# Pooled and banded attention with a gated MLP on one core: one batch instead of two on TensorE by groups, no fill matmuls, and a newly searched instruction order

## The chip, the cores and the metric

The kernel runs on one core of one Trainium2 chip. The metric is the device time of one execution in microseconds. The kernel before takes 767.54 us (median of 3 runs, 767.11 to 768.03). In what follows PE is TensorE, DVE is VectorE, ACT is ScalarE, POOL is GpSimd and SP is SyncE, which here only issues DMAs.

## The reference, cut to what matters

Attention over 8 batches and 8 heads (576 tokens, head dimension 64) is the sum of two softmax attentions: one over q, k and v averaged over four neighbouring tokens and then repeated four times, and one over the band of keys fewer than 4 tokens away. The result, 4608 rows of 512, goes through a gated MLP without an activation function.

```python
def _attn_ref(q, k, v) -> np.ndarray:
    ...
    q_d = q.reshape(B, H, Sd, factor, D).mean(axis=3)
    ...
    out_up = np.repeat(sm_attn(q_d, k_d, v_d), factor, axis=2)
    mask = np.abs(pos[:, None] - pos[None, :]) < factor
    scores = np.where(mask, scale * np.matmul(q, k.transpose(0, 1, 3, 2)), -1000000000.0)
    ...
    return (out_up + np.matmul(attn, v)).astype(np.float32)

def _moe_ref(x, w1, w2, w3, w_out) -> np.ndarray:
    a = x @ w1
    b = x @ w2
    h = a * b @ w3
    return (h @ w_out).astype(np.float32)
```

## The kernel before

**The work and its pieces.** The 4608 rows are cut into 24 units of 192 rows (a third of a batch each), and two units make a chunk of 384 rows, so there are 12 chunks, numbered 0 to 11. A batch `b` gives units `3*b` to `3*b+2`. For every unit the band attention is computed, the pooled attention of its batch is added, and the sum is written as two parts, `xh` (the high bits) and `xl` (the rest), so that three fp32r matmuls replace one exact one (`three`, L308 to L310). The MLP of a chunk (`moe`) has eight blocks: for each, 24 gate matmuls into `pab` (12 with w1, 12 with w2), then ACT copies `a` out (L1006), DVE multiplies (L1008), ACT takes the high part `gh` (L1013), DVE the low part `gl` (L1015), and 9 down matmuls accumulate into `acc`. w3 and w_out are multiplied together first (`fold`: L412 on PE, result `wphl`), and all weights arrive as float64 words that ACT and DVE turn into floats (L340, L348, L352, L355).

**Two ways to do the band.** A unit outside the batches in `PB` is done by `unit`: q times each of 7 shifted k on DVE (`pr`, L858), sums over the head dimension on DVE (L871) or ACT (L868), a softmax over 7 values (L878 to L893), 7 weighted v on DVE (`pv`, `xl`, L924) or ACT (L916), three of the six additions on DVE (L934) and three by accumulating DMAs on POOL's queue (L932), then a transpose (L938), the pooled part (L945), `xh` (L951) and `xl` (L952). A unit of a batch in `PB` is done by `group_unit`: score matmuls for groups of 16 pooled positions (`se_ps`, L743), mask, maximum, exponent and division on DVE and ACT (L754 to L770), transposes (`te_ps`, L713), value matmuls (`oe_ps`, L786), the pooled part (L795), `xh` and `xl` (L803, L804). Its batch also has its q and k summed over four tokens on DVE (`pooled_sums`, L646 to L674) instead of by accumulating DMAs (L505).

```python
        if n in rests:
            rests[n](n)
        else:
            unit(n)
        if n == 1:
            fold()
            for g in range(3):
                gate_weights(g)
        if n % 2:
            moe(n // 2)
```

**What sets the order.** Every piece is one task of a planner, and the task's place on its engine comes from a table of numbers, `ORDER`, one list for each of ACT, DVE, PE, Pool and SP (L63 on). Each engine works strictly in that order; a task waits there until what it needs is ready, and everything behind it on the engine waits too. The tiles of `unit` live in a pool, `dvp`, that reuses the memory of the pool of the group units, `pep`: the loads of the first `unit` (`q_t`, `kv`) wait until all group work is over.

**Fills.** `warm(WARM)` gives PE 20 matmuls on zeros before the weights arrive. `keep_clock(m, n)` (L395) adds n more, whose zero product goes into an accumulator of the fold, at the places in `IDLE`.

```python
PB = (0, 1)
IDLE = ((3, 1, 10), (4, 1, 15), (6, 1, 2))
```

Of the kernel before, what the change touches and what calls it, by code (L numbers as in the profile page):

```python
# [43 lines left out]
PB = (0, 1)  # L44
# [14 lines left out]
IDLE = ((3, 1, 10), (4, 1, 15), (6, 1, 2))  # L59
# [37 lines left out]
    ),  # L97
    DVE=(
# [1078 lines left out]
```

## Time and profile before

| | |
|---|---|
| median of 3 runs | 767.54 us |
| span of the profiled execution | 764.2 us |
| PE, DVE, ACT, POOL busy | 749.3, 611.3, 543.7, 128.4 us |
| PE weight loads busy | 652.7 us |
| HBM read and written | 80.26 and 9.44 MB |

The span runs from the first to the last instruction; the runs' times are those of whole executions, and their median is 3.3 us longer than this span. Busy time is the time in which at least one instruction of the engine runs, so that overlapping instructions count once. Matmuls overlap, and the duration of one is longer than the distance to the next.

### The profile page before, as it was taken

What the parts mean: (1) busy time and instruction counts of PE and PEld (TensorE: products, weight loads), DVE (VectorE), ACT (ScalarE), POOL (GpSimd) and SP (SyncE); (2) the same over time, 40 slices, a digit from 0 to 9 for tenths busy, and PEclk for the clock granted to TensorE, in tenths of its full rate; (3) what the DMA queues carried; (4) which work ended last, traced back from release to release, by engine and by line L of the source; (5) the groups of instructions that cost most, each with busy time, mean ns of one, the idle gap of its engine ahead of it and who ended that gap; (6) DMA issues with size and microseconds to landing.
All of it is one profiled execution on the core that took longest, in us unless ns stands there. A gap on an engine that the chain in (4) does not pass through costs nothing.

```text
span 764.2 us, 14972 instructions
## 1 busy us (share of the span) xinstructions
PE 749.3 (98%) x5342; PEld 652.7 (85%) x5342; DVE 611.3 (80%) x1063; ACT 543.7 (71%) x2133; POOL 128.4 (17%) x163
## 2 busy tenths in 40 slices
PE   9999999999999999999999999999999999999996
PEld 6544598789999899899988989899998999999995
DVE  4786898457999999999979999999998999973111
ACT  5399769567778878969778689786788888751211
POOL 2120200310110320232012401331022310010000
PEclk9999999999999999999999999999999999999999
DMA  8998962743695555786479647965478644241101
GB/s 280 313 264 263 241 194 61 140 94 118 151 215 138 143 127 156 140 191 158 96 172 206 135 117 187 177 155 131 115 165 196 138 108 124 47 100 21 36 7 42
DMA packets 51463, 111.91 MB, mean 146 GB/s; under 512 B 5548, under 2 KB 19884, under 8 KB 51388
## 3 DMA queue, kind: packets, MB, share of 16 engines
q0 software_dynamic: 15360, 38.94, 30.0%
q1 hardware_dynamic: 35892, 71.75, 29.1%
q8 instruction: 42, 0.69, 0.4%
q14 instruction: 33, 0.27, 0.1%
q10 hardware_dynamic: 136, 0.26, 0.1%
HBM read 80.26 MB, written 9.44 MB: 117 GB/s over the span
## 4 chain that ended last, share of the span: by engine, by line
PE 80%; DMA 10%; ACT 4%; DVE 4%; issue 1%; SPq 0%; POOL 0%; ACTq 0%; DVEq 0%; POOLq 0%
PE pab L308 16%; PE pab L310 16%; PE pab L309 16%; PE acc L308 8%; PE acc L309 8%; PE acc L310 8%; DMA xl<-pv 3%; DMA raw<-in_w_dram 3%; DMA v_w<-in_v_dram 2%; PE s_ps L566 2%; PE o_ps L527 1%; PE t_ps L605 1%; DMA vs<-in_v_dram 1%; PE oe_ps L786 1%; PE accw L412 1%
## 5 line engine op out<-in xcount | busy, mean ns | idle before, releaser
L868 ACT ACTIVATE junk<-pr 128x64 f32<-128x64 f32 x432 | 111.1, 257 | 20.4 <-DVE pr L858 9.0
L916 ACT ACTIVATE pv<-kv,s 128x64 f32<-128x64 f32 x432 | 111.3, 339 | 12.7 <-DVE s L893 9.4
L858 DVE TENSOR_TENSOR pr<-q_t,kv 128x768 f32<-128x768 f32 x126 | 116.9, 950 | 1.0 <-DMA q_t<-in_q_dram 1.0
L308 PE MATMUL acc<-wphl,gh 128*128 128x512 f32 x288 | 114.5, 398 | 0.0
L310 PE MATMUL acc<-wphl,gl 128*128 128x512 f32 x288 | 112.8, 392 | 0.0
L309 PE MATMUL acc<-wphl,gh 128*128 128x512 f32 x288 | 112.8, 392 | 0.0
L932 POOL DMA_DIRECT2D xl<-pv x54 | 48.3, 894 | 360.1 <-DVE xl L934 311.1
L1008 DVE TENSOR_TENSOR a<-pab,a 128x384 f32<-128x384 f32 x96 | 53.2, 554 | 48.5 <-PE pab L310 33.7
L871 DVE TENSOR_REDUCE s<-pr 128x12 f32<-128x768 f32 x90 | 84.5, 949 | 1.0
L1006 ACT COPY a<-pab 128x384 f32<-128x384 f32 x96 | 45.7, 476 | 53.0 <-PE pab L310 46.4
L1013 ACT CAST gh<-a 128x384 fp32r<-128x384 f32 x96 | 48.9, 510 | 45.2 <-PE acc L309 36.9
L868 ACT ACTIVATION_READ_ACCUMULATOR junk<-pr 128x1 f32 x432 | 81.1, 188 | 0.0
L1015 DVE TENSOR_TENSOR gl<-a,gh 128x384 fp32r<-128x384 f32 x96 | 52.8, 552 | 26.5 <-ACT gh L1013 26.0
L924 DVE TENSOR_TENSOR pv<-kv,s 128x768 f32<-128x768 f32 x72 | 67.8, 949 | 0.3
L308 PE MATMUL pab<-xh,w1a 128*128 128x384 f32 x192 | 65.4, 341 | 0.6 <-ACT a L1006 0.6
L308 PE MATMUL pab<-xh,w2a 128*128 128x384 f32 x192 | 64.9, 338 | 1.1 <-ACT a L1006 1.1
L308 PE MATMUL pab<-xh,wb 128*128 128x384 f32 x192 | 65.6, 342 | 0.0
L308 PE MATMUL pab<-xh,wo 128*128 128x384 f32 x192 | 65.2, 339 | 0.1
L310 PE MATMUL pab<-xh,wb 128*128 128x384 f32 x192 | 64.5, 336 | 0.0
L310 PE MATMUL pab<-xh,wo 128*128 128x384 f32 x192 | 64.5, 336 | 0.0
L309 PE MATMUL pab<-xl,wb 128*128 128x384 f32 x192 | 64.5, 336 | 0.0
L310 PE MATMUL pab<-xh,w1a 128*128 128x384 f32 x192 | 64.4, 336 | 0.0
(122 smaller groups left out, 1737.3 us busy)
## 6 DMA issues: line engine op xcount, KB each, us to landing
xl<-pv POOLq DMA_DIRECT2D x54, 384.0 KB, 4.8
raw<-in_w_dram SPq DMA_DIRECT2D x32, 512.0 KB
qks<-in_qk_dram POOLq DMA_DIRECT2D x18, 576.0 KB, 8.0
kv<-in_kw_dram SPq DMA_DIRECT2D x18, 576.0 KB
kv<-in_vw_dram SPq DMA_DIRECT2D x18, 576.0 KB
out_dram<-o_sb SPq DMA_DIRECT2D x29, 256.0 KB
q_t<-in_q_dram SPq DMA_DIRECT2D x18, 384.0 KB
raw<-in_wout_dram SPq DMA_DIRECT2D x8, 512.0 KB
```

The source lines that it names most:

```text
L308: nc.tensor.matmul(out_ps, lhsT=lh, rhs=rh, start=first, stop=False)
L309: nc.tensor.matmul(out_ps, lhsT=lh, rhs=rl, start=False, stop=False)
L310: nc.tensor.matmul(out_ps, lhsT=ll, rhs=rh, start=False, stop=last)
L858: (nc.gpsimd if o in share["qk_pool"] else nc.vector).tensor_tensor(out=T[o], in0=T["q"], in1=T["k"][:, o * D:o * D + nq].rearrange("p (t ...
L868: nc.scalar.activation(out=junk, in_=T[o][:, t], func=AF.Copy, accum_out=T["s"][:, t, o:o + 1])
L871: reds.append(add("DVE", dve_us(nq), lambda o=o: nc.vector.tensor_reduce(out=T["s"][:, :, o], in_=T[o], op=ALU.add, axis=AX.X), [tp], uses ...
L916: nc.scalar.mul(out=T["pv", o][:, tt], in_=T["v"][:, (tt + o) * D:(tt + o + 1) * D], mul=T["s"][:, tt, o:o + 1])
L924: nc.vector.tensor_tensor(out=T["pv", o], in0=T["v"][:, o * D:o * D + nq].rearrange("p (t d) -> p t d", d=D), in1=T["s"][:, :, o].unsqueez ...
L932: t = add("Pool", 0.9, lambda o=o: nc.gpsimd.dma_start(out=T["x"], in_=T["pv", o], accum_op=ALU.add), [t, tm], uses=[hx, h], late=dma_us(1 ...
L1008: tg = add("DVE", dve_us(CT), lambda f=f: nc.vector.tensor_tensor(out=T["a", f], in0=T["p", 1, f], in1=T["a", f], op=ALU.mult), [ta, ends[ ...
L1013: nc.scalar.copy(out=T["gh", f], in_=T["a", f])
L1015: tl = add("DVE", dve_us(CT), lambda f=f: nc.vector.tensor_tensor(out=T["gl", f], in0=T["a", f], in1=T["gh", f].bitcast(F32), op=ALU.subtr ...
```

## The change

`PB` loses batch 1: its three units, 3 to 5, are done by `unit` on DVE and ACT, and its q and k are summed by accumulating DMAs, as for batches 2 to 7. `IDLE` is empty, so the 54 fill matmuls of L395 go; the first 20 on zeros stay. All five lists of `ORDER` are new. Nothing else differs; lines below the table stand four lines further down.

```diff
-PB = (0, 1)
+PB = (0,)
...
-IDLE = ((3, 1, 10), (4, 1, 15), (6, 1, 2))
+IDLE = ()
...
     ACT=(
-        "64 63 65-67 69 68 70-72 74 73 75-79 0-1 3-5 2 81 80 82-86 7 11 6 9 87 17 15 14 13 12 10 88-89 16 24 26 25 94 27 8 95 29 91 30 28 "
...
+        "63 65 64 66-67 69 68 71 70 72-78 5 79 2 80-82 84 83 0 86 85 87 24-25 27 26 3-4 30 89 88 94 6 29 95 28 96 7 15 31 97-98 32 92 100 "
...
```

Three places show what the new lists do. The first is SP, where the loads of the first `unit` stand (`q_t`, `kv`), behind the group units' values (`v_w`). Before:

```order
L696 DMA v_w<-in_v_dram 72x1x512 x3
L486 DMA qks<-in_qk_dram 128x1152
L490 DMA vs<-in_v_dram 72x512
L491 DMA vs<-in_v_dram 56x512
L492 DMA vl<-in_v_dram 16x512
L696 DMA v_w<-in_v_dram 36x1x512 x2
L696 DMA v_w<-in_v_dram 72x1x512 x4
L1043 DMA out_dram<-o_sb 128x512
L1043 DMA out_dram<-o_sb 64x512 x2
L1043 DMA out_dram<-o_sb 128x512
L836 DMA q_t<-in_q_dram 128x768
L840 DMA kv<-in_kw_dram 128x1152
```

And now:

```order
L700 DMA v_w<-in_v_dram 36x1x512 x2
L700 DMA v_w<-in_v_dram 72x1x512
L337 DMA raw<-in_w_dram 128x2x512 x6
L700 DMA v_w<-in_v_dram 72x1x512 x3
L337 DMA raw<-in_w_dram 128x2x512 x2
L494 DMA vs<-in_v_dram 72x512
L495 DMA vs<-in_v_dram 56x512
L496 DMA vl<-in_v_dram 16x512
L840 DMA q_t<-in_q_dram 128x768
L844 DMA kv<-in_kw_dram 128x1152
L848 DMA kv<-in_vw_dram 128x1152
```

The loads of the first `unit` now follow the last weights (`raw`) and the values of the third group unit, ahead of all stores of the output; the values of three more group units are gone from in front of them.

The second place is DVE, from the last low part of a group unit (`xl` from `xf`) to the first product of a `unit` (`pr`). Before, where it is the sixth group unit and chunk 2 is complete:

```order
L804 TENSOR_TENSOR xl_2058<-xf,xh_2057 128x2x192
L572 TENSOR_SCALAR gmx<-gmx 128x4
L1008 TENSOR_TENSOR a<-pab,a 128x384
L588 TENSOR_SCALAR gsm<-gsm 128x4
L589 RECIPROCAL gsm<-gsm 128x4
L1015 TENSOR_TENSOR gl<-a,gh 128x384
L596 TENSOR_TENSOR pexp<-pexp,gsm 128x2x16
L1008 TENSOR_TENSOR a<-pab,a 128x384
L1015 TENSOR_TENSOR gl<-a,gh 128x384
L858 TENSOR_TENSOR pr<-q_t,kv 128x768 x3
```

And now, where it is the third group unit, in the middle of the blocks of chunk 0:

```order
L808 TENSOR_TENSOR xl_1289<-xf,xh_1288 128x2x192
L592 TENSOR_SCALAR gsm<-gsm 128x4
L593 RECIPROCAL gsm<-gsm 128x4
L600 TENSOR_TENSOR pexp<-pexp,gsm 128x2x16
L1019 TENSOR_TENSOR gl<-a,gh 128x384
L1012 TENSOR_TENSOR a<-pab,a 128x384
L575 TENSOR_REDUCE gmx<-s_ps 128x3 x2
L576 TENSOR_SCALAR gmx<-gmx 128x6
L862 TENSOR_TENSOR pr<-q_t,kv 128x768 x3
```

The first product has moved from the end of batch 1's group work to the end of batch 0's, with about as little other work between.

The third place is PE, where the gates of chunk 9 begin (`xh_7087` before, `xh_6912` now). Before, they follow the last gates of chunk 8 (`xh_6295`):

```order
L309 MATMUL pab<-xl_6296,wb 128x384
L310 MATMUL pab<-xh_6295,wb 128x384
L308 MATMUL pab<-xh_7087,w1a 128x384
L309 MATMUL pab<-xl_7088,w1a 128x384
L310 MATMUL pab<-xh_7087,w1a 128x384
```

And now they follow the last down matmuls of chunk 8:

```order
L312 MATMUL acc_6698<-wphl,gh 128x512
L313 MATMUL acc_6698<-wphl,gh 128x512
L314 MATMUL acc_6698<-wphl,gl 128x512
L312 MATMUL pab<-xh_6912,w1a 128x384
L313 MATMUL pab<-xl_6913,w1a 128x384
L314 MATMUL pab<-xh_6912,w1a 128x384
```

Before, 0.29 of chunk 8's down matmuls were left for later, among the gates of chunk 9. Now every chunk's down matmuls all stand ahead of the next chunk's gates, at all eleven boundaries.

## Rows read from the trace of the kernel before

**Rows 1.** The page's first part, busy time of each engine with its share of the span, and two rows of its second part, the busy tenths of DVE and PE in 40 equal slices of the span.

```profile
PE 749.3 (98%) x5342; PEld 652.7 (85%) x5342; DVE 611.3 (80%) x1063; ACT 543.7 (71%) x2133; POOL 128.4 (17%) x163
PE   9999999999999999999999999999999999999996
DVE  4786898457999999999979999999998999973111
```

**Rows 2.** Busy time of each engine by stage: the stretch and its length, then PE, weight loads, DVE, ACT, POOL with their counts, the granted clock, the busy share of the DMA engines and GB/s. The cuts are the start of the MLP of chunk 0, the first `pr` of a `unit`, and the moments at which `xl` of chunks 5 and 9 was written; the last row begins with the gates of chunk 1.

```profile
0.00:93.60 93.60, 89.36 (x710) 50.43 (x711) 65.52 (x160) 66.97 (x174) 20.52 (x37) 1.00 0.93 273
93.60:180.10 86.50, 85.88 (x1044) 75.08 (x1044) 56.69 (x151) 59.66 (x211) 10.19 (x12) 1.00 0.53 138
180.10:372.60 192.50, 192.50 (x1214) 177.41 (x1213) 184.25 (x284) 156.72 (x684) 36.87 (x43) 1.00 0.61 143
372.60:592.30 219.70, 216.91 (x1420) 197.35 (x1422) 204.18 (x318) 175.42 (x744) 45.39 (x53) 1.00 0.70 159
0.00:592.30 592.30, 584.64 (x4383) 500.28 (x4387) 510.63 (x907) 458.76 (x1811) 112.96 (x145) 1.00 0.68 169
...
163.70:764.20 600.50, 589.82 (x3780) 541.38 (x3777) 495.87 (x773) 426.93 (x1777) 97.66 (x114) 1.00 0.55 129
```

**Rows 3.** The instructions in order of time (start, length, engine, line, operation): the second low part of chunk 9 on DVE, the first gate matmul of chunk 9 on PE, and the last two down matmuls of chunk 11.

```profile
591.34 0.96 DVE L952 TENSOR_TENSOR xl<-xt,xh 128x768 fp32r<-128x768 f32 x1 [0.39 <-ACT xh L951]
...
597.41 0.34 PE L308 MATMUL pab<-xh,w1a 128*128 128x384 f32 x1
...
756.32 0.39 PE L309 MATMUL acc<-wphl,gh 128*128 128x512 f32 x1
756.54 0.39 PE L310 MATMUL acc<-wphl,gl 128*128 128x512 f32 x1
```

**Rows 4.** The chain of waits between 106 and 116 us, where group matmuls of batch 1 stand in it (start, length on the chain, what), and the group of the fill matmuls (busy time in all, mean ns of one).

```profile
106.08 0.90 PE se_ps L743 x23
...
110.37 0.65 PE te_ps L713 x6
...
114.84 1.48 PE oe_ps L786 x96
...
L395 PE MATMUL accw<-ident,still 128*128 128x128 f32 x54 | 6.6, 277 | 0.0
```

**Rows 5.** PE's instructions in order of time at three moments of the opening: the first matmuls on zeros, the fold where it waits for a weight, and the value matmuls of the second group unit where they wait for `v_w`.

```profile
1.13 7.59 PE L387 MATMUL accw<-still 128*128 128x128 f32 x40 [1.13 <-DVE still L290]
...
34.51 1.98 PE L412 MATMUL accw<-wo,w 128*128 128x512 f32 x4 [1.36 <-DVE w L355]
...
86.44 1.32 PE L786 MATMUL oe_ps<-pte,v_w 72*32 72x64 f32 x80 [0.60 <-DMA v_w<-in_v_dram]
```

**Rows 6.** Groups of DVE instructions of a `unit`, 18 units in all: first the products and the sums, then the longest of the eight groups of 768 columns, then two of the softmax's small steps (count, busy time, mean ns of one).

```profile
L858 DVE TENSOR_TENSOR pr<-q_t,kv 128x768 f32<-128x768 f32 x126 | 116.9, 950 | 1.0 <-DMA q_t<-in_q_dram 1.0
L871 DVE TENSOR_REDUCE s<-pr 128x12 f32<-128x768 f32 x90 | 84.5, 949 | 1.0
L938 DVE STREAM_TRANSPOSE xt<-xl 128x768 f32<-128x768 f32 x18 | 17.5, 972 | 1.2 <-DMA xl<-pv 1.1
L890 DVE TENSOR_REDUCE sm<-s 128x12 f32<-128x96 f32 x18 | 4.5, 248 | 1.2 <-ACT s L886 1.2
L892 DVE RECIPROCAL sm<-sm 128x12 f32<-128x12 f32 x18 | 4.1, 228 | 0.5
```

**Rows 7.** Groups of DVE instructions of the two batches done by groups: the five longest and the shortest of fourteen.

```profile
L754 DVE TENSOR_TENSOR se<-se_ps,band 128x216 f32<-128x216 f32 x24 | 8.2, 376 | 3.6 <-PE se_ps L743 3.5
L795 DVE TENSOR_TENSOR xf<-oe_ps,oup 128x192 f32<-128x192 f32 x24 | 7.5, 352 | 9.5 <-PE oe_ps L786 8.9
L770 DVE TENSOR_TENSOR se<-se,esm 128x432 f32<-128x432 f32 x12 | 7.3, 605 | 0.2
L763 DVE TENSOR_REDUCE emx<-se 128x6 f32<-128x432 f32 x12 | 7.2, 598 | 0.3
L804 DVE TENSOR_TENSOR xl<-xf,xh 128x384 fp32r<-128x384 f32 x12 | 6.7, 556 | 2.3 <-ACT xh L803 2.2
...
L509 DVE COPY vl<-vl 16x512 f32<-16x512 f32 x2 | 0.8, 418 | 0.1
```

**Rows 8.** DVE in order of time at the hand-over from groups to units: the last low part of a group unit, and the first three products of a `unit`.

```profile
171.87 0.55 DVE L804 TENSOR_TENSOR xl<-xf,xh 128x384 fp32r<-128x384 f32 x1
...
180.14 2.69 DVE L858 TENSOR_TENSOR pr<-q_t,kv 128x768 f32<-128x768 f32 x3
```

**Rows 9.** What DVE waited for (us in total, times, longest): three rows of the stretch from 180 to 592.3 us, and the first row of the stretch from 180 to 372.6 us.

```profile
DVE a L1008 <- PE pab L310: 5.9, 11, 1.0
DVE xl L934 <- DMA xl<-pv: 4.4, 2, 3.4
DVE gl L1015 <- ACT gh L1013: 2.2, 5, 0.6
...
DVE a L1008 <- PE pab L310: 2.9, 5, 1.0
```

**Rows 10.** The accumulating DMAs of the units, from the page's sixth part: count, size, median us from issue to landing.

```profile
xl<-pv POOLq DMA_DIRECT2D x54, 384.0 KB, 4.8
```

**Rows 11.** Two stretches of 1 us behind the last matmul, columns as in rows 2.

```profile
760.00:761.00 1.00, 0.00 (x0) 0.00 (x0) 0.00 (x0) 0.00 (x0) 0.00 (x0) 1.00 0.51 178
...
762.00:763.00 1.00, 0.00 (x0) 0.00 (x0) 0.00 (x0) 0.00 (x0) 0.00 (x0) 0.50 0.21 82
```

176 rows, old and new, of tables (ACT, DVE, PE, Pool) are left out of this document.

## The prediction

> **What bounds the kernel now.** I read the page's first part, then the stages, then two engines in order of time. The first part shows PE busy 749.3 us of 764.2 and DVE 611.3 [rows 1]. The stages say where DVE's free time lies [rows 2]. Until 93.6 us, when chunk 0 begins, the DMA engines are at 0.93 and DVE idles 93.6 - 65.52 = 28.1 us: the opening is set by loads, and PE itself waits for a weight and for `v_w` [rows 5]. From 93.6 to 180.1 PE is full and DVE idles 29.8 us, because no `unit` may start before the groups of batch 1 are done. From 180.1 to 592.3 PE is full (409.4 of 412.2) and DVE nearly so: idle 8.25 of 192.5, then 15.5 of 219.7. At the end of that stretch `xl` of chunk 9 is ready at 592.3 and its gates start at 597.41 [rows 3]: 5.1 us spare. So PE sets the end, with DVE close behind it, and DVE's only large reserve is the stage before 180 us. The slices show DVE nearly empty again in the last 70 us [rows 1], but nothing can move there, since the MLP of chunk 11 needs all units done.
>
> **The change part by part.** *PE.* A group unit costs two score blocks of 0.90, two flips of 0.65 and one value block of 1.48: 4.58 us [rows 4]. Three go: 13.7 us. The fills go too, 6.6 us [rows 4], but they stand in the opening, beside the waits of 1.36 and 0.60 us [rows 5]; the bounds are 0 and 6.6, and I take 0, because the stage is set by loads and the nearest rows are waits. Had PE stayed the bound, the span would be 764.2 - 13.7 = 750.5, or 743.9 with the fills.
>
> *DVE.* A `unit` has 23 instructions of 768 columns, 0.949 to 0.972, and five small steps of about 0.24 [rows 6]: 23 x 0.951 + 5 x 0.24 + 0.1 (the edge mask, on two units of three) = 23.2 us, three of them 69.6. The group work of one batch is half of fourteen groups, of which the five longest and the shortest are shown [rows 7]; count times mean over all of them gives, for one batch, 31.8. Net 37.8 us. These are summed lengths, and neighbours overlap: three products of 0.950 take 2.69 [rows 8], and over the whole engine counts times means give 668.8 against 611.3 busy [rows 1], a factor 0.914. So DVE gets 34.5 us more to do, and what hid such work before, PE's lead, is the 5.1 us above.
>
> *Where it decides.* I count to the moment when `xl` of chunk 9 is ready. Before, DVE had been busy 510.6 us by then [rows 2]. In the new list 42.8 summed us more stand ahead of it (the 37.8, and 5 of work for later units that now comes earlier), 39.1 in busy time: 549.7. From the gates of chunk 9 to the end it took 764.2 - 597.4 = 166.8. In the new list 6.5 less is left for PE there: 0.29 of a chunk's 72 down matmuls, one every 0.228 on average (the last two start 0.22 apart [rows 3]), 4.8 us, and 1.7 of pooled attention, now stand ahead. That leaves 160.3. With 0.3 from the last low part to the first gate, span = 549.7 + 160.3 + 0.3 + idle = 710.3 + DVE's idle time before that moment. (The same sum for the kernel before: 510.6 + 81.7 idle + 5.1 + 166.8 = 764.2.)
>
> The idle time has three parts. The opening: its loads are almost the same, so 28, with 24 and 30 as bounds; chunk 0 then begins near 87 to 89. The hand-over: the first `unit` loads after the last group unit, and before that took from 171.87 to 180.14, 8.3 us [rows 8], in which DVE had 2.6 of other work; the new list has 2.7 there, so 5.6, and 2.4 for the waits for the third group unit's matmuls: 8. The rest, 463 us busy from the first product to chunk 9: in 180.1 to 372.6, with PE full, DVE idled 8.25, of which 2.9 was waiting for PE's gates [rows 9]. Once DVE is the late one, such waits should mostly go, so 5.3 of 192.5, 2.8%: 13.3 us. Bounds: 2%, 9.4; and the 5.8% of the whole stretch to 592.3 (23.8 of 412.2, waits for PE and all [rows 2]), 28.5.
>
> Sum: 710.3 + 28 + 8 + 13.3 = 759.6. The same path through chunk 1 gives 761: it needs 68.6 busy us after chunk 0's low part, plus 8 and 1, while PE has some 59 us of work for it, so PE should stand idle there for 12 to 16 us; from chunk 1's gates to the end it took 600.5 [rows 2], now 4.7 less by count (87 + 77.6 + 0.3 + 595.8). The two agree within my error. The median of the runs is 767.54, 3.3 above the span, so 759.6 means 762.9: I say 763.
>
> *Hidden.* POOL gets nine more accumulating DMAs of `unit` and three more sums of q and k; it was busy 128.4 us [rows 1], and the DMA engines were at 0.61 to 0.70 after 180 us [rows 2], so bandwidth costs nothing; their latency is a rival. ACT gains 32 summed us by count, some 25 busy, to 543.7 [rows 1] and stays below DVE. On SP, the loads of the first `unit` stand behind eight weight loads and three `v_w`, which must have gone out for the group unit anyway.
>
> **The rivals.** *PE stays the bound.* DVE keeps ahead, because the new lists are made for its load, idling under 1.5%, and chunks come in time. Then the floor above holds, 743.9 to 750.5, in runs 747 to 754. For it: PE without a gap over 192 us [rows 2]. Against: DVE would have to do 34.5 us more in a time 14 shorter, and the hole before chunk 1.
>
> *DVE's waits are not PE's fault (slower).* A unit's three accumulating DMAs hang on one another, 4.8 us each from issue to landing [rows 10]; DVE waited for them 4.4 us and for `gh` from ACT 2.2 [rows 9], at a time when PE held it back and a wait cost nothing. With three more units, and batch 1's sums of q, k and v in between in POOL's queue, DVE stands in these waits with nobody behind to hide them. At 4.3% (all its waits of 180 to 592 but the 5.9 for PE) the third part is 20.8 and a run takes 770.4; at 5.8%, 778. It decides from 4.0%, where a run takes 769.1.
>
> *Nothing to see.* The third part comes to 3.4 to 4.0%, 16.4 to 19.5 us, or the opening loses what the rest gains: 766 to 769, the 13.7 us of PE bought and paid back on DVE.
>
> *The clock.* Behind the last matmul, which ends at 756.9, the granted clock is still 1.00 at 760 and 0.50 at 762 [rows 11], that is 1.2 GHz for 2.4. So the hole before chunk 1 can drop it. Forty matmuls on zeros at the start, most of them at the lower level, took 7.59 us, 0.19 each [rows 5], against 6.6 / 54 = 0.12 for the fills [rows 4]: a drop costs about 40 x 0.07 = 2.7 us. One is hidden while DVE is late. One at each of eleven boundaries, since every chunk now ends with its own down matmuls, would take 30 us: PE's 743.9 to 750.5 become 774 to 780, 777 to 784 in runs. The Trainium skill's page "TensorE: Matmul & The Clock Gate", section "Why this matters for your kernels", warns of idle gaps between bursts of matmuls in mid-kernel, since they put the array back to the slower clock. By that rule taking out fills speaks against the change; the trace agrees in its one long gap, at the end, and shows no drop at the gap of 1.36 us, where the stage's clock is 1.00 [rows 2].
>
> **How the numbers follow.** Faster or slower is told from no change at 0.2%: under 766.0, over 769.1. The forecast, DVE as the bound, 758 to 766: 0.37. PE the bound, 747 to 754, and the space up to 758: 0.17. Nothing to see: 0.18. DVE's waits: 0.25. The clock: 0.03. Faster 0.54, same 0.18, slower 0.28. The range goes from 750 to 775; what it leaves out is the lower half of PE's case and the far ends of the last two. The forecast's own range is 758 to 766.
>
> **What would show it.** Right: PE idle some 23 us up to its last matmul, instead of 756.9 - 749.3 = 7.6, above all 12 to 16 us near 150 to 165, and short gaps where chunks begin; gates starting within 1 us of `xl`; the first product of a `unit` near 122 instead of 180; DVE busy about 646 us and its stages from there above 0.96. Wrong: if PE shows no gaps and `xl` is ready several us before the gates, PE stayed the bound; if DVE's waits for `xl` and `gh` grow past 4%, the slower case; if the first product comes after 130, the hand-over was mis-sized.

## The result and the profile after

The changed kernel takes 772.2 us (median of 4 runs, 771.36 to 773.04), the kernel before, timed beside it, 767.33 (764.55 to 768.03): ratio 1.0065, 95% interval 1.0036 to 1.0094. It is slower; I had forecast 763.0, faster. Three later timings of the same kernel, on three chips, gave 1.0126 (1.0092 to 1.0160), 1.0108 (1.0068 to 1.0148) and 1.0064 (1.0034 to 1.0095). The profiled execution has a span of 769.6 us, 2.6 below the median.

The first part of the profile's page and two rows of its second part, of the kernel after (they answer to [rows 1]; PEclk is the granted clock in tenths):

```profile
PE 739.9 (96%) x4820; PEld 641.0 (83%) x4820; DVE 638.2 (83%) x1066; ACT 558.1 (73%) x2266; POOL 139.2 (18%) x175
DVE  5845778999999999999989999979989989976111
PEclk9998999979999999999999999999999999999999
```

PE lost 20.3 us of work by the prediction's count and shows only 9.4 less busy time (749.3 to 739.9); DVE is full from 125 us on; and the clock has two slices below 9, where before it had none.

Busy time by stage after, columns as in [rows 2]. The cuts are `xl` of chunk 0, the first `pr`, and `xl` of the chunks 1, 5 and 9; the last row begins with the gates of chunk 9:

```profile
0.00:91.00 91.00, 81.71 (x624) 43.80 (x625) 57.03 (x145) 64.08 (x167) 14.41 (x30) 0.96 0.89 265
91.00:125.50 34.50, 32.24 (x310) 26.70 (x309) 26.75 (x60) 25.21 (x72) 3.26 (x4) 1.00 0.61 181
125.50:168.40 42.90, 37.14 (x234) 30.55 (x233) 40.70 (x64) 37.47 (x174) 10.48 (x12) 0.88 0.79 182
168.40:386.00 217.60, 216.24 (x1361) 197.84 (x1360) 209.65 (x333) 179.42 (x792) 51.53 (x61) 1.00 0.71 161
386.00:608.20 222.20, 218.34 (x1428) 198.58 (x1427) 208.03 (x325) 172.49 (x760) 48.33 (x57) 0.99 0.67 152
...
609.40:769.60 160.20, 152.99 (x866) 142.60 (x864) 94.85 (x143) 78.40 (x302) 10.89 (x13) 0.99 0.31 74
```

Behind the stretch and its length stands PE's busy time, and as the third of the busy times DVE's. The prediction's sum was made of these terms, and they are now measured:

| term (us) | predicted | measured |
|---|---|---|
| DVE busy until `xl` of chunk 9 | 549.7 | 542.2 |
| from there to the gates of chunk 9 | 0.3 | 1.2 |
| gates of chunk 9 to the end | 160.3 | 160.2 |
| DVE idle: opening (0 to 91.0) | 28 | 34.0 |
| DVE idle: hand-over (91.0 to 125.5) | 8 | 7.75 |
| DVE idle: the rest (125.5 to 608.2) | 13.3 (2.8%) | 24.3 (5.0%) |
| span | 759.6 | 769.6 |

PE has an account of its own. The same view cut at the gates of chunk 1 and at the last matmul, of the kernel before:

```profile
0.00:163.70 163.70, 159.46 (x1565) 111.35 (x1566) 115.47 (x291) 116.80 (x356) 30.70 (x49) 1.00 0.76 210
163.70:756.90 593.20, 589.79 (x3780) 541.38 (x3777) 495.79 (x773) 426.35 (x1776) 97.66 (x114) 1.00 0.56 129
```

and of the kernel after:

```profile
0.00:169.70 169.70, 152.39 (x1170) 102.12 (x1171) 125.78 (x267) 128.06 (x418) 28.30 (x47) 0.95 0.80 225
169.70:762.40 592.70, 587.47 (x3651) 538.91 (x3649) 512.39 (x800) 429.50 (x1848) 110.91 (x129) 1.00 0.59 135
```

Ahead of chunk 1 PE stood idle 17.3 us instead of 4.2 and ran at half clock, 1.2 GHz for 2.4, in two stretches of 6.9 and 10.2 us, in which it was busy 15.9 us. At most half of that, 7.9 us, is lost to the clock, so by this estimate the work there fell by 15.0 us (159.5 to 152.4 - 7.9 = 144.5), and chunk 1 still began 6.0 us later. Behind it PE's busy time fell by 2.3 us and the stretch by 0.5. So in these two profiles the last matmul came 5.5 us later: 6.0 lost ahead of chunk 1, 0.5 won behind it. Some three quarters of what PE was relieved of stood ahead of chunk 1, whose gates also need DVE's low part of the first `unit`: it was written at 168.4, and they began at 169.7.

The hole ahead of the first half-clock stretch, the three stretches themselves, and the 15 us in which the prediction had PE idle for 12 to 16 (it was idle 4.6), columns as above:

```profile
62.60:67.20 4.60, 0.00 (x0) 0.00 (x0) 3.75 (x9) 3.44 (x11) 0.00 (x0) 1.00 0.94 265
67.20:74.10 6.90, 6.86 (x73) 4.11 (x74) 2.51 (x9) 3.75 (x10) 0.00 (x0) 0.51 0.62 195
...
156.00:166.20 10.20, 9.03 (x78) 5.90 (x77) 9.39 (x17) 7.66 (x30) 0.86 (x1) 0.50 0.65 171
...
524.60:528.00 3.40, 3.40 (x12) 3.35 (x11) 3.06 (x5) 3.34 (x16) 1.85 (x3) 0.51 0.81 133
...
150.00:165.00 15.00, 10.39 (x92) 7.27 (x91) 14.30 (x23) 11.61 (x54) 1.73 (x2) 0.70 0.77 167
```

Each half-clock stretch comes behind a hole on PE. PE's instructions in order of time (start, length, what, idle time before and what ended it): the three holes, the first gates of the chunks 0, 1 and 9, and the last matmul.

```profile
67.24 1.19 PE L531 MATMUL o_ps<-pt,vs 128*32 128x144 f32 x16 [4.64 <-DMA vs<-in_v_dram]
...
94.76 0.74 PE L312 MATMUL pab<-xh,w1a 128*128 128x384 f32 x1
...
154.61 0.44 PE L609 MATMUL t_ps<-ident,pexp 128*128 128x128 f32 x2 [3.44 <-ACT pexp L598]
...
169.73 0.34 PE L312 MATMUL pab<-xh,w1a 128*128 128x384 f32 x1
...
524.07 0.44 PE L312 MATMUL pab<-xh,wo 128*128 128x384 f32 x1 [2.02 <-DVE a L1012]
...
609.39 0.34 PE L312 MATMUL pab<-xh,w1a 128*128 128x384 f32 x1
...
762.00 0.39 PE L314 MATMUL acc<-wphl,gl 128*128 128x512 f32 x1
```

On DVE, in order of time: the first product of a unit ([rows 8] showed it at 180.14), and the last low parts of the chunks 1 and 9 (answering to [rows 3]).

```profile
125.49 0.96 DVE L862 TENSOR_TENSOR pr<-q_t,kv 128x768 f32<-128x768 f32 x1
...
167.43 0.96 DVE L956 TENSOR_TENSOR xl<-xt,xh 128x768 fp32r<-128x768 f32 x1
...
607.28 0.95 DVE L956 TENSOR_TENSOR xl<-xt,xh 128x768 fp32r<-128x768 f32 x1
```

What DVE waited for between 170 and 605 us after, the first three rows and a later one (answering to [rows 9]):

```profile
DVE xl L938 <- DMA xl<-pv: 8.0, 4, 3.6
DVE a L1012 <- PE pab L314: 1.8, 3, 0.9
DVE gl L1019 <- ACT gh L1017: 1.4, 4, 0.5
...
DVE pr L862 <- DMA q_t<-in_q_dram: 0.8, 1, 0.8
```

Waits for PE's gates went from 5.9 to 1.8 us, as predicted; waits for the accumulating DMAs went from 4.4 to 8.0 (in a window of 435 us instead of 412), though one of them now takes 4.2 us from issue to landing, where [rows 10] have 4.8.

What DVE waited for in the opening, until `xl` of chunk 0: the three longest rows before (to 93.6 us) and after (to 91.0), all of them waits for ACT's share of the weights' conversion:

```profile
DVE wo L355 <- ACT wo L340: 8.5, 3, 5.3
DVE wx L355 <- ACT wx L340: 3.6, 3, 1.9
DVE w L355 <- ACT w L340: 3.2, 5, 1.0
...
DVE w L359 <- ACT w L344: 9.1, 6, 3.0
DVE wo L359 <- ACT raw L352: 6.9, 1, 6.9
DVE wx L359 <- ACT wx L344: 6.4, 2, 4.3
```

### The profile page after: what moved, and what is told of

Read it like the earlier page. It is cut to its first block, busy times and chain, and to the rows that moved or that the text cites. A ratio compares the mean times of both kernels' runs of the same rounds, so it can differ in the third digit from the quotient of the medians.

```text
span 769.6 us, 14109 instructions
## 1 busy us (share of the span) xinstructions
PE 739.9 (96%) x4820; PEld 641.0 (83%) x4820; DVE 638.2 (83%) x1066; ACT 558.1 (73%) x2266; POOL 139.2 (18%) x175
## 4 chain that ended last, share of the span: by engine, by line
PE 51%; DMA 17%; DVE 13%; ACT 9%; issue 5%; POOL 1%; SPq 1%; DVEq 0%; ACTq 0%; POOLq 0%
PE pab L312 10%; PE pab L314 10%; PE pab L313 10%; PE acc L312 6%; PE acc L314 6%; PE acc L313 6%; DMA vs<-in_v_dram 5%; DMA raw<-in_w_dram 4%; ACT junk L872 4%; DVE pr L862 4%; PE o_ps L531 2%; DMA xl<-pv 2%; DVE s L875 1%; DMA vl<-in_v_dram 1%; DMA raw<-in_wout_dram 1%
## 5 line engine op out<-in xcount | busy, mean ns | idle before, releaser
L920 ACT ACTIVATE pv<-kv,s 128x64 f32<-128x64 f32 x504 | 132.7, 337 | 15.2 <-DVE s L897 8.9
L872 ACT ACTIVATE junk<-pr 128x64 f32<-128x64 f32 x504 | 129.1, 256 | 16.0 <-DVE pr L862 4.7
L862 DVE TENSOR_TENSOR pr<-q_t,kv 128x768 f32<-128x768 f32 x147 | 135.3, 949 | 2.0 <-ACT junk L872 0.9
L875 DVE TENSOR_REDUCE s<-pr 128x12 f32<-128x768 f32 x105 | 97.9, 946 | 0.3
L872 ACT ACTIVATION_READ_ACCUMULATOR junk<-pr 128x1 f32 x504 | 94.8, 188 | 0.0
L928 DVE TENSOR_TENSOR pv<-kv,s 128x768 f32<-128x768 f32 x84 | 78.5, 949 | 1.3 <-DMA xl<-pv 0.8
L938 DVE TENSOR_TENSOR xl<-xl,pv 128x768 f32<-128x768 f32 x63 | 59.9, 951 | 17.6 <-DMA xl<-pv 12.2
L493 POOL DMA_DIRECT2D vs<-in_v_dram x48 | 50.4, 1150 | 93.1 <-DMA vs<-in_v_dram 91.3
L312 PE MATMUL pab<-xh,w1a 128*128 128x384 f32 x192 | 65.9, 343 | 0.7 <-ACT a L1010 0.5
L313 PE MATMUL pab<-xl,wo 128*128 128x384 f32 x192 | 65.1, 339 | 0.0
```

Of the source, the lines that this page charges most:

```text
L312: nc.tensor.matmul(out_ps, lhsT=lh, rhs=rh, start=first, stop=False)
L313: nc.tensor.matmul(out_ps, lhsT=lh, rhs=rl, start=False, stop=False)
L493: dma = (lambda **kw: nc.gpsimd.dma_start(accum_op=ALU.add, **kw)) if add else nc.sync.dma_start
L862: (nc.gpsimd if o in share["qk_pool"] else nc.vector).tensor_tensor(out=T[o], in0=T["q"], in1=T["k"][:, o * D:o * D + nq].rearrange("p (t ...
L872: nc.scalar.activation(out=junk, in_=T[o][:, t], func=AF.Copy, accum_out=T["s"][:, t, o:o + 1])
L875: reds.append(add("DVE", dve_us(nq), lambda o=o: nc.vector.tensor_reduce(out=T["s"][:, :, o], in_=T[o], op=ALU.add, axis=AX.X), [tp], uses ...
```

## The experiments

Two theories stood at the start. *DVE sets the end* (the prediction's): each us of DVE's work or waits is one of the span, and the loss is the opening and the waits. *PE sets the end*: the holes and the half clock are lost time. A ratio is always to the kernel before, timed beside it on one chip; the groups of runs were on different chips, so kernels of different groups are compared with care. A profile is of one execution.

**The opening: loads and fills.** `o_ps` of batch 0 waits for `vs` and `vl`, whose first loads stand on SP behind 19 weight loads (the expectation says 20). First these loads were moved forward.

```diff
-21-22 5 23-27 6-7 28-31 12 32-38
+21-22 5 12 23-27 6-7 28-38
```

> The changed kernel with one task moved on SP: the first loads of batch 0's values (vs, vl) go out right behind the last of its k4 loads instead of behind 20 weight loads. Loads theory (the late loads make o_ps wait 4.6 us on PE, and DVE, which sets the end, starts its units that much later): o_ps starts near 63 instead of 67.2, no stretch at half clock there, gates of chunk 0 near 90 instead of 94.8, first product of a unit near 121 instead of 125.5, time 4 to 5 us shorter, 767 to 768. PE theory (PE sets the end and the hole counts directly): 3 to 5 us shorter as well, but gates of later chunks then start well behind xl. Fills theory (clock drops for want of fills are the loss): the clock still drops in the opening and the time is within 1 us of the changed kernel's.

Ratio 1.0045 (1.0013 to 1.0077), span 765.1. The hole went, but `o_ps` did not come earlier:

```profile
67.76 0.70 PE L531 MATMUL o_ps<-pt,vs 128*32 128x144 f32 x16
```

PE was busy with products of the fold up to that moment, so the loads theory is wrong as it stood. What changed is the clock: these matmuls took 0.70 us instead of 1.19, and chunk 0's gates came 24.0 us behind `o_ps` (91.8) instead of 27.5 (94.8); chunk 1's at 164.4. Then the fills were put back, with the loads as in the changed kernel:

```diff
-IDLE = ()
+IDLE = ((3, 1, 10), (4, 1, 15), (6, 1, 2))
```

> The changed kernel with the 54 fill matmuls put back behind the products of block 1 with j = 3, 4 and 6. Fills theory: the stretches at half clock go and the time falls by 3 to 5 us. Loads theory: o_ps still waits for vs and vl until 67, the clock still falls behind that wait, the fills lie ahead of it and cost PE 5 to 7 us that it has spare: within 1 us of the changed kernel. PE theory: about 6 us longer.

Ratio 1.0043 (1.0013 to 1.0073), span 770.0. `o_ps` at 67.4 at full clock, chunk 0 at 91.8, chunk 1 at 164.9, all as in the run before; but from there to the end it took 605.1 us, where the changed kernel's four profiles have 599.9 to 603.4. And the fills taken from the kernel before:

> The kernel before without its 54 fill matmuls, all else in place. Fills theory: slower than before by 3 to 5 us, with a stretch at half clock between 30 and 60 us. PE theory: up to 6 us shorter, since PE sets the end and has less to do. Loads theory: within 1 us, because loads set the opening and the fills lie beside waits for them.

Ratio 1.0023 (0.9997 to 1.0049): no difference that can be told. Its profile, of the slowest of its 12 runs, shows half clock at 28.5 to 31.9, 35.3 to 42.2 and 93.4 to 96.8 us, where the kernel before has none, and chunk 0's gates at 100.7 instead of 93.3. To separate the hole from the clock, 34 fills were put into the hole itself, and the changed kernel was run beside it.

```diff
+            if b == 0:
+                for _ in range(34):
+                    nc.tensor.matmul(open_acc[5][:, :128], lhsT=still, rhs=ident, start=False, stop=False)
```

> The changed kernel with 34 fill matmuls (some 4.1 us) on PE right ahead of o_ps of batch 0, that is inside the hole of 4.6 to 5.7 us, and nothing else. Clock theory (the wait itself is cheap, the half clock behind it costs): o_ps still starts at 67 to 68, takes 1.97 us instead of 3.44, gates of chunk 0 come near 92 instead of 95, those of chunk 1 3 to 5 us earlier, time 3 to 5 us shorter than the changed kernel of the same call. Wait theory (the hole itself is the loss): o_ps and all behind it within 1 us of the changed kernel's.

> The changed kernel as it is, a third timing, to compare the other runs of this call with. All theories: ratio to before between 1.004 and 1.013.

1.0112 (1.0066 to 1.0158) against 1.0108 (1.0068 to 1.0148). The hole and the stretch behind it in this run:

```profile
62.60:67.20 4.60, 4.60 (x44) 4.60 (x43) 2.51 (x6) 1.86 (x5) 0.00 (x0) 1.00 1.01 295
67.20:74.10 6.90, 6.90 (x93) 4.59 (x92) 2.13 (x6) 3.46 (x10) 0.00 (x0) 1.00 0.48 150
```

So the clock theory is right on what it says of PE (25.5 us from `o_ps` to chunk 0's gates, 32.5 in the changed kernel beside it; chunk 1 at 164.0 against 173.6), and the time did not follow: from chunk 1 on it took 605.1 us against 601.6, and the two ratios are equal. The two profiles are of executions of 770.9 and 777.0 us, so not all of the 9.6 us at chunk 1 need be the hole's.

A further step took the third group unit's `v_w` and batch 1's first `vs` ahead of the last four weight loads, in the belief that the memory of the first unit comes free only when those weights are converted. What the profiles show is the load of `q_t` waiting for the low part of the third group unit, 9.9 us in the changed kernel and 9.6 in this run.

```diff
-45-50 56-58 51-52 60-63
+45-48 56-58 60 49-52 61-63
```

> The changed kernel with two moves on SP alone: the first loads of batch 0's values right behind the k4 loads (as in the earlier run), and the third group unit's v_w and batch 1's first vs and vl ahead of the last four weight loads instead of between and behind them. Hand-over theory (the last weights release the memory of the first unit, whose first product so starts at 122 to 127; from there DVE has no time to give): last weight conversions at 109 to 110 instead of 113 to 117, first product near 118, gates of chunk 1 near 161, end 4 us before that of the run with the first move alone, time 764 to 766. Balance theory (behind chunk 1 PE and DVE are both full and the gain is lost in new waits): first product near 118 too, but the end within 1.5 us of the run with the first move alone.

Ratio 1.0025 (0.9998 to 1.0052), span 764.4. First product at 121.5, not 118, chunk 1 at 163.9. The price of moving loads was misjudged, the gain over the first move is not shown. It was run again beside the changed kernel:

> The changed kernel as it is, on one chip with the run below. All theories: ratio to before between 1.005 and 1.013.

> The run with the two moves of loads on SP once more, beside the changed kernel on the same chip, since the chips differ. Opening theory (what is lost ahead of chunk 1 reaches the end): gates of chunk 1 4 to 6 us earlier than in the changed kernel's profile, time 0.4 to 0.7% shorter than the changed kernel's. Balance theory: chunk 1 earlier by as much, but the time within 0.2% of the changed kernel's.

1.0042 (1.0016 to 1.0068) against 1.0064 (1.0034 to 1.0095): 1.8 us in the medians, with intervals that overlap; chunk 1's gates were 2.8 us earlier in the profiles. That is between the two theories and settles neither.

**One engine relieved at a time.** The addition of the pooled part in `up` was left out, in the changed kernel and in the kernel before:

```diff
-            nc.vector.tensor_tensor(out=x, in0=x, in1=o, op=ALU.add)
+            pass
```

> The changed kernel without the addition of the pooled part in the units (one DVE instruction of 768 columns, some 0.87 us net, in each of 21 units; that part of the output is left out). DVE theory (DVE sets the end): 17 units stand ahead of chunk 9, so the time falls by 10 to 15 us, to 757 to 762, and PE's gaps shrink. PE theory: within 2 us.

> The kernel before without the addition of the pooled part in its 18 units (that part of the output is left out), the control for the run that did this to the changed kernel. All theories hold that PE sets the end of the kernel before: within 2 us of before, DVE some 13 us less busy and waiting that much longer.

Changed: 1.0036 (1.0007 to 1.0065), some 2 to 7 us better than the changed kernel's four timings, none of which ran beside it; its interval overlaps with two of theirs. Before: 1.0007 (0.9980 to 1.0035), nothing. Then 48 down matmuls, 11.0 us of PE by count; from chunk 1 to the end the profiles show PE 7.4 us less busy in the changed kernel (587.5 to 580.1) and 8.2 in the kernel before (589.8 to 581.6):

```diff
+                    if 2 <= c <= 9 and f in (3, 4):
+                        nc.tensor.matmul(T["acc"][i], lhsT=gh[:, cs], rhs=wphl[:, f, 0], start=False, stop=False)
+                        nc.tensor.matmul(T["acc"][i], lhsT=gl[:, cs], rhs=wphl[:, f, 0], start=False, stop=False)
+                        return
```

> The changed kernel without 48 of its down matmuls (the second of each three, for blocks 3 and 4 of the chunks 2 to 9; that small part of the product is left out): 48 times 0.229 us is 11.0 us less for PE between 220 and 660 us. PE theory (the holes and half-clock stretches ahead of chunk 1 are lost time, and from there PE sets the end): 8 to 11 us shorter. DVE theory (DVE sets the end from there as well): 0 to 2 us shorter, and PE's gaps grow by 9 to 11 us.

> The changed kernel as it is, timed once more beside the runs below. All theories: the ratio to before as in the first timing, 1.004 to 1.009.

> The kernel before without the same 48 down matmuls (that small part of the product is left out), the control for the run that did this to the changed kernel. If PE alone sets the end of the kernel before: 9 to 11 us shorter. If DVE is so close behind that it takes over at once: 3 to 6 us shorter, since xl of chunk 9 had 5.1 us to spare.

Changed: 1.0074 (1.0048 to 1.0100) against 1.0126 (1.0092 to 1.0160) beside it, 3.6 us of those 7.4, with intervals that just overlap; before: 0.9902 (0.9865 to 0.9939), 7.4 us of 8.2. And both cuts together:

> The changed kernel without the 48 down matmuls and without the addition of the pooled part in the units. Both theories: 9 to 13 us shorter than the changed kernel, since both engines have less to do. If a latency that hangs on neither (the accumulating DMAs, one after another) sets the pace: 0 to 5 us.

1.0017 (0.9988 to 1.0047), 8.6 us below the changed kernel beside it. The stretch from chunk 1's gates to those of chunk 9 shows what happened, each time in the profile of that run (length, then PE's busy time first and DVE's third). The kernel before, then without the 48 matmuls, then without `up`:

```profile
163.70:597.40 433.70, 430.29 (x2856) 393.59 (x2854) 400.16 (x623) 346.34 (x1476) 83.80 (x98) 1.00 0.65 152
```

```profile
164.70:591.60 426.90, 423.02 (x2815) 385.06 (x2814) 398.78 (x623) 345.01 (x1474) 83.39 (x98) 1.00 0.65 154
```

```profile
165.00:600.50 435.50, 431.77 (x2857) 395.33 (x2855) 388.65 (x609) 346.51 (x1476) 83.92 (x98) 1.00 0.65 151
```

PE's idle time is 3.4, 3.9 and 3.7 us: the stretch is nearly all PE's work. The changed kernel, then without the matmuls, without `up`, and without both:

```profile
169.70:609.40 439.70, 434.48 (x2787) 396.31 (x2786) 417.58 (x658) 351.68 (x1549) 100.02 (x117) 1.00 0.69 156
```

```profile
166.50:607.10 440.60, 427.69 (x2743) 387.91 (x2744) 417.55 (x659) 353.00 (x1557) 99.87 (x116) 1.00 0.69 156
```

```profile
166.30:605.30 439.00, 433.21 (x2786) 394.61 (x2786) 407.05 (x644) 352.91 (x1557) 100.33 (x117) 1.00 0.69 157
```

```profile
170.10:603.70 433.60, 424.64 (x2745) 386.56 (x2743) 406.19 (x644) 352.37 (x1556) 99.92 (x116) 1.00 0.70 158
```

The stretch keeps its length when PE gets less (PE's idle time goes from 5.2 to 12.9 us) and when DVE gets less (DVE's from 22.1 to 31.9), and shortens by 6.1 only when both do. Single profiles scatter, so two more without either cut, the changed kernel's fourth timing and the run with the filled hole:

```profile
171.20:614.40 443.20, 435.85 (x2786) 396.48 (x2787) 419.52 (x660) 353.74 (x1558) 100.64 (x117) 1.00 0.68 155
...
164.00:608.60 444.60, 435.43 (x2786) 394.26 (x2785) 419.15 (x660) 353.30 (x1556) 100.01 (x117) 1.00 0.68 155
```

Against 439.7 to 444.6 us, one cut alone (440.6 and 439.0) cannot be told from none, and 433.6 stands clear. Neither of the two theories holds alone: both engines stand so near their limit that each bounds the other. Other engines are in it too: in the run without the 48 matmuls PE's longest wait behind chunk 1, 3.9 us before 293.9 for a product of DVE, follows a wait of DVE of 3.9 us that ends at 289.8 behind a copy on ACT.

**Is there a third bound?** The last of a unit's three accumulating DMAs was left out, alone and with both cuts.

```diff
-lambda o=o: nc.gpsimd.dma_start(out=T["x"], in_=T["pv", o], accum_op=ALU.add), [t, tm]
+(lambda: None) if i == 6 else lambda o=o: nc.gpsimd.dma_start(out=T["x"], in_=T["pv", o], accum_op=ALU.add), [t, tm]
```

> The changed kernel without the last of a unit's three accumulating DMAs (that part of the weighted sum is left out); work of PE, DVE and ACT as before. Latency theory (behind chunk 1 the three DMAs that hang on one another set the pace, with little to spare on PE and DVE): 4 to 8 us shorter, DVE's waits for xl<-pv gone or halved. Balance theory (PE, 99% busy there, and DVE, 95%, bound each other): 0 to 3 us shorter.

> The changed kernel without the 48 down matmuls, without the addition of the pooled part in the units, and without the last accumulating DMA. With the first two left out the time was 1.1% shorter, of 11 and 14 us that PE and DVE had less to do. Latency theory: now the rest comes, 4 to 6 us more. Balance theory: within 2 us of the run with the first two.

1.0152 (1.0119 to 1.0185), not faster than the changed kernel beside it (1.0108), rather slower; and 1.0049 (1.0016 to 1.0083) with both cuts, no better than without this one (1.0017). Between the two runs without the third DMA, timed side by side, both cuts again gave 8.7 us (medians 778.6 and 769.8). What DVE waited for between 170 and 605 us in the first of them:

```profile
DVE xl L938 <- DMA xl<-pv: 8.7, 3, 4.4
DVE pr L862 <- DMA q_t<-in_q_dram: 6.4, 3, 2.5
DVE a L1012 <- PE pab L314: 3.1, 5, 1.0
DVE pr L862 <- DMA kv<-in_kw_dram: 2.0, 1, 2.0
```

A third of the accumulating DMAs went and the waits for the others stayed (8.7 us), while waits for the loads of `q_t`, 0.8 us in the changed kernel, grew to 6.4, and those for `kv` came on top. The latency of these DMAs as the pace is not borne out.

**Two holes closed by hand.** PE waited 3.44 us for the last divisions of batch 1's second pooled block, and 2.02 us for a product in chunk 7, at the same places in nearly every profile of this order. On top of the two moves of loads both instructions were put forward in the lists of ACT and DVE:

```diff
-211 236 164-165 237 267 238 265 239-241 264 242 210 263 270 268 273 266 212
+211 210 212 236 164-165 237 267 238 265 239-241 264 242 263 270 268 273 266
...
-817-818 774 808 775 718 717
+817-818 718 717 774 808 775
```

> The kernel of the run before this one, with two more moves: on ACT the last two divisions of batch 1's second pooled block ahead of unit 3's products (PE waited 3.44 us for them near 151 in every run), and on DVE the product a of chunk 7's block 3 and the low part before it three places earlier (PE waited 2.03 us near 522 in every run). Balance theory: each gap goes and little of it reaches the end, 0 to 2 us. PE theory: 5 us less, and the half-clock stretch near 155 gone.

Ratio 1.0051 (1.0028 to 1.0074), against 1.0025 without these edits on the same chip: no gain. PE's instructions at the two places:

```profile
153.22 0.69 PE L531 MATMUL o_ps<-pt,vs 128*32 128x144 f32 x4 [4.34 <-ACT pt L618]
...
527.26 0.50 PE L314 MATMUL acc<-wphl,gl 128*128 128x512 f32 x1 [2.59 <-DVE gl L1019]
```

Both holes went and were paid a few instructions later, 4.34 us for the copies of `pt` and 2.59 for a low part. With the fills on top:

> The same with the 54 fills put back. Clock theory (a hole in the opening drops the clock and chunk 0's gates come some 3 us late; fills prevent it): no half-clock stretch before chunk 0, gates of chunk 0 no later than without fills, 0 to 3 us shorter. Fills only cost where no hole is left: 0 to 3 us longer.

Ratio 1.0067 (1.0042 to 1.0092): no gain either, and half clock at 85.0 to 91.8 and 156.7 to 166.9 all the same. No version of the changed kernel beat the kernel before. The six timings with loads moved or fills put back have ratios of 1.0025 to 1.0067, the changed kernel's four 1.0064 to 1.0126, but the filled hole has 1.0112, and only one of the six ran beside the changed kernel: that a better opening gains something is suggested, not shown.

## Why the prediction was wrong, step by step

- *The sign.* Wrong. The median is 9.2 us above the forecast of 763.0; the time lies in the range of 750 to 775.
- *DVE becomes the late one, and gates start within 1 us of `xl`.* The lag at chunk 9 is 1.2 us. But that it is then the bound, as the sum supposed, failed. From chunk 1's gates to the last matmul PE was busy 587.5 of 592.7 us, and of the 5.2 it waited none was for `xl`. Relieved of 14.2 us ahead of chunk 9 on DVE (542.2 to 528.0 busy) the kernel gained 2 to 7 us, if anything, and relieved of 7.4 us on PE some 4. I compared DVE's path with PE's floor and took the longer one; where both are near full, in-order lists make the time longer than either.
- *"Once DVE is the late one, such waits should mostly go", 2.8% idle.* This is the step that cost most: 5.0%, 24.3 us instead of 13.3. The waits for PE did go (5.9 to 1.8 us). Others came: accumulating DMAs 8.0 for 4.4. I had taken the idle share from the better of two stages, 180.1 to 372.6: the next one, to 592.3, had 15.5 of 219.7 us, 7.1%, before, and the stage that answers to it has 14.2 of 222.2, 6.4%, after. The rival on DVE's waits had named this place and 4.0% as its point. Its cause was named too narrowly: taking a third of these DMAs away only moved the waits to loads.
- *The opening, 28 us.* Mis-sized: 34.0, outside its bounds of 24 to 30. "Its loads are almost the same" overlooked that on SP batch 0's values had moved from behind 11 weight loads to behind 19, which shows in PE's hole of 4.64 us. That is half of it: with this load moved forward, or with the fills back, DVE's idle time until `xl` of chunk 0 was 31.2 and 31.4 us. The longest waits there, for ACT's share of the weights, went from 15.3 to 22.4 us (three rows each); why is open. In the changed kernel's four profiles `xl` of chunk 0 comes at 91.0 to 95.7.
- *Hand-over 8, first product near 122.* 7.75 and 125.5; the difference is the opening's. *Chunk 1 by its own path* had 77.6 us from `xl` of chunk 0 to that of chunk 1: 77.4. But its last part, 595.8 from chunk 1's gates to the end, took 599.9: PE's busy time there fell by 2.3 us, not by the 4.7 of the count.
- *DVE busy until chunk 9, 549.7.* 542.2. DVE's busy time in all rose by 26.9 us (611.3 to 638.2), not by 34.5 to about 646, and its stages stood at 0.95, 0.96 and 0.94, not above 0.96. Counts times means with the factor for overlaps overstated the term by 7.5, which hid part of the error.
- *Gates of chunk 9 to the end, 160.3.* 160.2. *PE idle some 23 us, above all 12 to 16 near 150 to 165.* 22.5 up to the last matmul, but this is luck: between 150 and 165 it was 4.6, of which 3.4 was a wait for ACT's `pexp`, and 9.3 lay in the opening.
- *Fills worth 0, bounds 0 and 6.6.* Taken out alone they cost nothing that can be told (1.0023, up to 1.0049). Put back into the changed kernel they left `o_ps` at full clock, and the time moved by less than the changed kernel's own timings differ.
- *The clock, 0.03, "one is hidden while DVE is late".* The drops came, 20.5 us of half clock in three stretches, in which PE was busy 19.3 us: at most 9.6 lost, 3.2 a drop where 2.7 was forecast. The Trainium skill's page "TensorE: Matmul & The Clock Gate", section "Why this matters for your kernels", warns of idle gaps between bursts of matmuls in mid-kernel, and here the trace agrees behind holes of 4.64 and 3.44 us; the one of 2.02 us is shorter than those it names. That most of it is hidden fits the filled hole, whose ratio equals the changed kernel's, with intervals of some 3 us either way. Its chance was too small for the event, its price about right, though not by its working: from 1 to 9 us, where the prediction put most of the forty matmuls at the lower level, the granted clock reads 1.00. The better row is `o_ps`, 3.44 us instead of 1.97 for the same work.
- *Where PE's 20.3 us went.* Some 15 of them, by the estimate above, lay ahead of chunk 1 and turned into idle time and half clock there. What is shown: PE's account in the profiles, and that behind chunk 1 neither engine, relieved alone, gives its time back. What stays open: how much of the time won ahead of chunk 1 reaches the end, and so the cause of the whole 5 us. One pair on one chip says none, another 1.8 us, and neither interval decides.

## What to carry to other kernels

When work moves from the engine that bounds a kernel to one that stands 5 us behind it, do not take the maximum of the two: ask what both together do, since a wait of either now counts. The quickest test for it is to leave some work out on one engine, then on the other, in both kernels: an engine that alone sets the pace gives nearly all of it back (PE 7.4 of 8.2 us before, 3.6 of 7.4 after). And look stage by stage at where the saved work stands: here some three quarters of it stood ahead of chunk 1, whose gates needed another engine's work as well.

## What was not expected of the hardware

- Behind holes of some 2 us the granted clock fell in some executions and not in others: behind the 2.02 us at 522 the granted clock was 0.51 for 3.4 us in the first profile, and behind 2.03 us at the same place in the second one it stayed at 1.00; there it fell behind one of 1.93 us near 121. At half clock 64 matmuls of `o_ps` took 3.44 us instead of 1.97.
- Single executions of the changed kernel range from 768.2 to 779.9 us, and its ratio to before from 1.0064 to 1.0126 over four timings, while the kernel before had medians of 766.3 to 767.3 us beside it. Its four profiles have holes of 4.6 to 6.3, 3.4 and 2.0 us at the same instructions, and half-clock stretches at other places in each, with the same instructions in the same order.
